# Two heads' scores at once in row halves, with the selection as a multiplied mask, for the last two of four sequences

## The chip, the cores and the metric

The kernel runs on one core of a Trainium2 chip. The metric is the device time in microseconds (us) of one launch; the time before is the median of three runs, 265.23 us (264.53 to 265.60).

## What is computed

Two stages follow each other. The first is causal attention over 4 sequences (B) of 768 tokens (S), 8 heads (H) of 64 channels (D), in which each query may look only at six of the 24 chunks of 32 keys. Which six is decided by an upper bound for each chunk, from the smallest and the largest key of the chunk in each channel:

```python
k_min, k_max = min and max of k over each chunk of 32 keys
ub = sum over channels of max(q * k_min, q * k_max)        # one number for query and chunk
ub = where(chunk of the key <= chunk of the query, ub, -1e9)
top_chunks = the 6 chunks with the largest ub
scores = q @ k.T / 8, -1e9 where the chunk isn't selected or the key lies behind the query
attn = softmax(scores);  x = attn @ v                       # heads side by side: [3072, 512]
h = max(x @ w_in, 0)                                        # w_in  [512, 2048]
out = (h * h) @ w_out                                       # w_out [2048, 512]
```

The second stage, the last two lines, is a feed-forward part over all 3072 tokens. Inputs and output are float32; the kernel computes in bf16 with float32 sums.

## The kernel before

**Tiles and units.** A tile is 128 tokens, so a sequence has six (NT). The first tile of every sequence needs no selection, since it has only four chunks; `first_attention` does it for all four sequences early on, with plain causal attention. The other five tiles (NS) are done by pairs of heads: pair p is sequence p // 4 and heads 2 (p % 4) and 2 (p % 4) + 1, which lie in channels 0 to 63 and 64 to 127 of a 128-row tile. There are 16 pairs.

**Stage a of a pair (`stage_a`, L622)** prepares it. Keys and queries, transposed to channels x tokens (`kT`, `qT`), give the bounds: two reductions over chunks on VectorE (`kr`, L690), small matmuls (`ub`, L656 and L658), a mask for later chunks (`ubm`, L715), the eight largest of each row (`MAX8`, L664), and a comparison with the sixth (`selb`, L720), which gives 1 for each chunk that is *not* selected. That is transposed (`sT`) so that chunks lie on rows. For sequences 0 and 1 the transposes are matmuls on TensorE; for sequences 2 and 3 (BY_DMA = 2) keys, queries and `sT` are turned by DMA transposes on SP's queue (`turn_by_dma`, L395).

**How the selection enters the scores before.** The matrix of the scores has 88 rows: 64 channels and 24 rows for the chunks. In `kqs` ("kqc" in the profile) the 24 rows hold -32768 where the key lies in the chunk; in `qss` ("qsc") they hold the turned selection. So a score of a chunk that isn't selected gets -32768 added by the matmul itself. `kqs` and `qss` have four sets (NSET), used in turn by the pairs. For every pair, eight copies fill a set: the keys of each head (`kqc<-kT` or `kqc<-kt`), the queries (`qsc<-qT`, `qsc<-qt`), and four copies of the selection (`qsc<-sT`). They are done by VectorE, or by ScalarE where the plan says so (lines L291 and L289 in the profile, the two branches of `copy`).

**Stage b of a pair (`stage_b`, L759)** does one head after the other in five "banks" of 512 columns (BANKS): scores into one PSUM buffer `ps` (L775, two or so matmuls of 88 rows), the exponential into `e` on ScalarE (L797), the causal cut of the diagonal tiles on GpSimd (L755) or VectorE (L752), and the product with the values into `av` (L786; a 65th column of ones gives the sum of the row). After five banks `normalise` (L601) divides into `x`.

**The feed-forward part (`ffn`, L816)** runs once for the four first tiles together and once for the five other tiles of each sequence: tokens are turned (`xT`), multiplied with `w_in` (`ph`, L859), passed through relu (`ht`, L866 on ScalarE or L868 on VectorE), squared (`h`, L877), multiplied with `w_out` (`py`, L890), copied to `ob` and written out by SP (L903).

**What sets the order.** Nothing loops at run time. `Plan` collects every operation with the engines that it may run on, an estimated cost, a due time, what it needs and which buffers it uses, and then places one operation after the other: the one that can start first, and among those on one engine that can start within 0.01 us of it, the one with the earliest due time. Buffers of a tag are taken from a fixed number of slots (three `ps`, two `av`, six `e`, three `ob` and so on) when their first user starts, and given back after the last. The result is one fixed order of instructions for each engine; at run time an engine only waits for semaphores. GpSimd's queue (POOL) issues the loads that convert float32 to bf16, in the order in which they were declared; SP's queue issues transposes by DMA and the output. Due times come from a few numbers in `P` (`lead` for each pair, `due` and `rate` for the feed-forward parts); `shift` can move the due time of single operations and is empty. Until 30 us the plan fills idle time of TensorE with matmuls on a constant (`wt`, L537).

Of the kernel before, what the change touches and what calls it, by code (L numbers as in the profile page):

```python
# [218 lines left out]
def kernel(  # L219
# [30 lines left out]
    P = dict(lead=[29, 46, 59, 39, 24, 71, 13, 53, 78, 15, 28, 72, 60, 6, 47, 77],  # L250
             f_due=[165, -158, -474.97, -240.97], sp='K0 Q0 K1 Q1', rows=-1719,
             rows_after=0, up_due=-70.08, up_rate=7.25, half=4,
             due=[-19, -136, -15, 35], rate=[4.42, 7.43, 6.24, 5.06], va=12.05,
             vm=6.24, ra=0.55, h2=-1.49, later='k1 q1 v1 k2 q2 q3 v2 v3 k3', shift={},
             p0=-3220, wait=0.01,
             loads="Q3 k0 K3 q0 V0 V1 V2 K2 Q2 k1 i0 "
                   "V3 i3 q1 v0 i2 k2 v1 R2 q2 i1 v2 o0 q3 k3 o1 v3 o2 o3")
# [13 lines left out]
    psav = ctx.enter_context(tc.tile_pool(name="psav", bufs=1, space=PSUM))  # L271
    psf = ctx.enter_context(tc.tile_pool(name="psf", bufs=1, space=PSUM))

    plan = Plan({"tp": 1, "ps": 3, "av": 2, "ff": 2, "e": 6, "h2": NFI + 6, "ht": 3,
                 "ob": 3, "kq": 6, "nt": 6,
                 "vn": B - 1, "x": 2, "xT": 2,
                 "kr": 2, "qp": 2, "qm": 2, "ubm": 2, "m8": 2, "rc": 2}, lambda *a: keep_warm(*a), P["wait"])
    POOLS = {"tp": pst, "ps": pss, "av": psav, "ff": psf, "e": epool, "h2": hpool,
             "ht": hpool, "ob": opool, "vn": ld, "nt": ldt, "kq": tpool}
# [13 lines left out]
    def transpose(dst, src):  # L293
# [10 lines left out]
    kqs = consts.tile([KC, NSET, 2, S], BF16, tag="kqs", name="kqc")  # L304
    qss = consts.tile([KC, NSET, 2, QC], BF16, tag="qss", name="qsc")
    selbs = consts.tile([128, NSET, NT, 2, 32], BF16, tag="selbs", name="selb")
    kbds = consts.tile([128, NSET, 2, 2, NC], BF16, tag="kbds", name="kbd")
    firsts = {nm: consts.tile([128, B, H, D], BF16, tag=nm + "0", name=nm + "0")
              for nm in "kq"}
# [3 lines left out]
    x_first = work.tile([128, B, d_model], BF16, tag="x0", name="x0", bufs=1)  # L313
# [17 lines left out]

    def make_ubmask(_):

        last = (NS - 1) * 128 // CH
        behind = consts.tile([128, last + NC], F32, tag="behind")
        nc.vector.memset(behind, 0.0)
# [7 lines left out]
    def kq_rows(i):  # L344
# [5 lines left out]
        elif i == 1:  # L350
            nc.sync.dma_start(out=kqs[D:KC, 0, 1], in_=kqs[D:KC, 0, 0])
        else:
            nc.gpsimd.dma_start(
                out=kqs[D:KC, 1:].rearrange("c s hh j -> c (s hh) j"),
                in_=kqs[D:KC, 0, 0:1].to_broadcast([NC, 2 * NSET - 2, S]))
# [16 lines left out]
    def first_of(nm, b):  # L372
        return vfirst[:, b, :, 0:D] if nm == "v" else firsts[nm][:, b]
# [613 lines left out]
```

## Time and profile before

The profile is of one execution. Its span, from the first to the last instruction, is 262.1 us; the median of the runs is 265.23 us, so 3.1 us lie outside the span.

| | before |
|---|---|
| median of the runs (lowest, highest) | 265.23 us (264.53, 265.60) |
| span of the profiled execution | 262.1 us |
| DMA packets, bytes | 103733, 26.12 MB |
| queue of POOL (software), of SP (hardware): MB | 13.33, 12.36 |
| granted clock of TensorE | full in each slice |

How to read the lines of the profile: PE is TensorE's matmuls, PEld its weight loads, DVE VectorE, ACT ScalarE, POOL GpSimd, SP the queue that only issues transfers. A group is written as line, engine, operation, written tile <- read tiles, shapes and count, then the busy time in us and the mean of one in ns, then the idle time of the engine just before them and what ended it. A matmul's busy time includes its way through the array, so that consecutive ones overlap; what each costs is seen from how far apart they start. The chain of work that ended last is followed back from the last instruction, and its lines say for how long what was on it. In the windows, "DMA share" is the busy time of the transfers over that of sixteen engines; where two queues are active, it can be above 1.

### The profile page before, as it was taken

To read this page: it belongs to the slowest core of one execution; us is meant where nothing else is said; L and a number is where in the kernel's file an instruction comes from. 1 tells how busy PE (TensorE), PEld (TensorE's weight loads), DVE (VectorE), ACT (ScalarE), POOL (GpSimd) and SP (SyncE) were. 2 spreads that over 40 slices of the span, in tenths; PEclk is the share of its full clock that TensorE was granted. 3 is DMA by queue.
4 is the path that set the end of the run, shared out by engine and by line. 5 is a ranking of instruction groups with operands and counts; after the bars stand their busy time and mean duration, and the time that the engine had idled before them with its cause. 6 is when DMAs were issued, how large, how long until landed. Compare 5 with 4: busy or idle time off the path is not lost.

```text
span 262.1 us, 6645 instructions
## 1 busy us (share of the span) xinstructions
PE 254.6 (97%) x2435; PEld 168.2 (64%) x2457; DVE 192.2 (73%) x677; ACT 180.2 (69%) x369; POOL 109.4 (42%) x196
## 2 busy tenths in 40 slices
PE   8899999999999999999999999999999999999995
PEld 4678765756687666656786656657767576565443
DVE  5399999968999999999999995886778531254000
ACT  1589798856599888986799847768889351377112
POOL 8997999978416729993121011411103000000000
PEclk9999999999999999999999999999999999999999
DMA  8999999999982999999571011163000011200222
GB/s 134 168 176 187 143 186 166 185 155 195 185 119 46 115 129 175 145 153 134 102 147 57 0 56 43 59 120 94 0 3 0 3 40 40 84 1 0 83 80 80
DMA packets 103733, 26.12 MB, mean 100 GB/s; under 512 B 96332, under 2 KB 100708, under 8 KB 103700
## 3 DMA queue, kind: packets, MB, share of 16 engines
q0 software_dynamic: 75168, 13.33, 65.9%
q1 hardware_dynamic: 28532, 12.36, 22.2%
q8 instruction: 19, 0.31, 0.5%
q14 instruction: 14, 0.11, 0.1%
HBM read 27.26 MB, written 6.29 MB: 128 GB/s over the span
## 4 chain that ended last, share of the span: by engine, by line
PE 89%; ACT 3%; DMA 3%; DVE 2%; issue 1%; SPq 1%; POOL 0%; ACTq 0%; POOLq 0%
PE py L890 31%; PE ph L859 31%; PE ps L775 13%; PE av L786 7%; DMA raw<-in_q_dram 3%; PE wt L537 1%; PE xt L294 1%; ACT qsc L289 1%; ACT ht L866 1%; PE kT L294 1%; SPq L406 1%; PE ub L658 1%; DVE kr L690 1%; PE ub L656 1%; PE qT L294 1%
## 5 line engine op out<-in xcount | busy, mean ns | idle before, releaser
L859 PE MATMUL ph<-xT,w_in_sb 128*128 128x256 bf16 (+2 forms) x592 | 98.0, 304 | 0.5 <-ACT ht L866 0.2
L797 ACT ACTIVATE e<-ps 128x512 bf16<-128x512 f32 x160 | 86.6, 604 | 10.8 <-PE ps L775 6.3
L890 PE MATMUL py<-w_out_sb,h 128*128 128x512 bf16 (+2 forms) x378 | 88.2, 370 | 1.2
L755 POOL TENSOR_SCALAR_AFFINE_SELECT e<-e 128x128 bf16<-128x128 bf16 (+1 forms) x102 | 34.8, 353 | 88.4 <-ACT e L797 79.7
L859 PEld LDWEIGHTS <-w_in_sb 128*128 128x128 bf16 x592 | 55.4, 97 | 24.5 <-issue 1.8
L866 ACT ACTIVATE ht<-ph 128x256 bf16<-128x256 f32 (+2 forms) x122 | 54.9, 455 | 17.2 <-PE ph L859 13.5
L877 DVE TENSOR_TENSOR h<-ht 128x256 bf16<-128x256 bf16 (+2 forms) x148 | 47.4, 330 | 19.9 <-ACT ht L866 13.1
L890 PEld LDWEIGHTS <-h 128*128 128x128 bf16 x400 | 36.5, 98 | 33.1
L775 PE MATMUL ps<-qsc,kqc 88*128 88x128 bf16 (+1 forms) x320 | 54.4, 272 | 0.0
L289 ACT COPY ob<-py 128x512 f32<-128x512 f32 (+2 forms) x22 | 12.5, 568 | 37.3 <-PE py L890 37.2
L786 PEld LDWEIGHTS <-e 128*128 128x128 bf16 x640 | 31.8, 97 | 7.9 <-POOL e L755 0.9
L775 PEld LDWEIGHTS <-kqc 88*128 88x128 bf16 x320 | 27.0, 98 | 11.9 <-issue 0.2
L786 PE MATMUL av<-vn,e 128*128 128x65 bf16 x480 | 32.0, 193 | 0.2 <-POOL e L755 0.2
L606 DVE TENSOR_TENSOR x<-av,rc 128x320 bf16<-128x320 f32 (+1 forms) x40 | 18.6, 470 | 0.3
L690 DVE TENSOR_REDUCE kr<-kT 128x24 bf16<-128x768 bf16 x16 | 14.8, 948 | 1.4 <-PE kT L294 1.4
L664 DVE MAX8 m<-ubm 128x8 f32<-128x24 f32 x160 | 15.6, 169 | 0.0
L690 DVE TENSOR_REDUCE kr<-kt 128x24 bf16<-128x768 bf16 x16 | 14.9, 944 | 0.0
L868 DVE TENSOR_SCALAR ht<-ph 128x256 bf16<-128x256 f32 (+2 forms) x26 | 12.2, 471 | 3.7 <-PE ph L859 3.6
L289 ACT COPY qsc<-sT 24x384 bf16<-24x384 bf16 (+1 forms) x32 | 14.1, 440 | 0.8
L786 PE MATMUL av<-v,e 128*128 128x65 bf16 x160 | 14.0, 193 | 0.0
L454 POOL DMA_DIRECT2D vn<-in_v_dram x15 | 13.3, 901 | 0.5 <-issue 0.5
L537 PE MATMUL wt<-warm 128*128 128x256 bf16 x73 | 11.5, 301 | 1.1 <-DVE warm L358 1.1
(84 smaller groups left out, 251.3 us busy)
## 6 DMA issues: line engine op xcount, KB each, us to landing
out_dram<-ob SPq DMA_DIRECT2D x23, 256.0 KB, 2.3
w_in_sb<-in_moe_w_in_dram POOLq DMA_DIRECT2D x4, 512.0 KB, 7.6
w_out_sb<-in_moe_w_out_dram POOLq DMA_DIRECT2D x4, 512.0 KB, 8.3
vn<-in_v_dram POOLq DMA_DIRECT2D x15, 128.0 KB, 5.7
nt<-in_k_dram POOLq DMA_DIRECT2D x10, 128.0 KB, 5.4
nt<-in_q_dram POOLq DMA_DIRECT2D x10, 128.0 KB, 5.7
kn<-in_k_dram POOLq DMA_DIRECT2D x8, 80.0 KB, 6.7
qn<-in_q_dram POOLq DMA_DIRECT2D x8, 80.0 KB, 6.7
```

The lines of the kernel that those rows point to most:

```text
L289: nc.scalar.copy(dst, src)
L606: return plan.op({"DVE": 0.06 + 0.00108 * D * n}, due, lambda _: nc.vector.tensor_mul(x(), av[:, :, 0:D], rc[:, 0:n].unsqueeze(2).to_broad ...
L664: nc.vector.max(out=m8[:, i, hh], in_=ubm[:, i, hh])
L690: nc.vector.tensor_reduce(kr[:, mm].rearrange("d (t c) -> d t c", c=128 // CH) if b >= BY_DMA else kr[:, mm], part(kT).rearrange("d t (c j ...
L755: nc.gpsimd.affine_select(out=e, in_=e, compare_op=ALU.is_ge, fill=0.0, base=0, channel_multiplier=-1, pattern=[[0, n], [1, 128]])
L775: nc.tensor.matmul(ps[:, 128 * c:128 * (c + nt)], lhsT=kqs[:, s, hh, 128 * j:128 * (j + 1)], rhs=qss[:, s, hh, 128 * (t0 - 1):128 * (t0 - ...
L786: nc.tensor.matmul(av[:, t - 1], lhsT=e[:, 128 * c:128 * (c + 1)], rhs=value_tile(b, h, j), start=(i == 0 and c == 0), stop=(i == len(BANK ...
L797: nc.scalar.activation(e.tile, ps.tile, ACT.Exp, scale=scale), [sc], [ps, e])
L859: nc.tensor.matmul(ph.tile, lhsT=w_in_sb[:, ki, 128 * f:128 * (f + 1)], rhs=xT[:, c0 // 128:c1 // 128, ki], start=(ki == 0), stop=(ki == N ...
L866: nc.scalar.activation(ht.tile, ph.tile, ACT.Relu)
L877: {"DVE": 0.067 + w / 1920}, at[0] + P["h2"], lambda _: nc.vector.tensor_mul(h2[f][:, c0:c1], ht.tile, ht.tile), [op], [ht, h2[f]])))
L890: nc.tensor.matmul(py.tile, lhsT=h2[f][:, 128 * t:128 * (t + 1)], rhs=w_out_sb[:, f, c0:c1], start=(f == 0), stop=(f == NFI - 1))
```

## The change

In sequences 2 and 3 (pairs 8 to 15), `stage_b_rows` takes the place of the loop over heads in `stage_b`.

- *Scores.* There is no `kqc` and no `qsc` for these pairs. The matmuls read the turned keys and queries directly, 64 rows for each head: the first head in rows 0 to 63, the second in rows 64 to 127, one after the other for every stretch of columns, each into a PSUM buffer of its own. They come in three groups (HELD): banks 0 and 1 of both heads, banks 2 and 3, bank 4. A group of two banks takes all three `ps` buffers and the `tp` buffer.
- *Selection.* `selb` holds 1 for a selected chunk now (is_ge for is_lt). It is turned by a DMA transpose of two instead of three blocks, written to DRAM by a DMA (`rowm`), and read back by six DMAs on SP's queue, one for each key tile, each of which copies four rows (the four chunks of the key tile) to 32 partitions each. The result is `keep`: 20 tiles of keys x queries for two heads. GpSimd cuts the five diagonal tiles of it causally. The reads of a pair wait for the last read of the pair before (`held_back`).
- *Product.* VectorE multiplies each `e` of 128 x 512 by its part of `keep` after the exponential; the causal cut of `e` goes for these pairs.
- *Room.* `kqs` and `qss` have three sets (KSET) instead of four. `keep` has two slots, in which at first the keys of the first tiles (`k0`) and the queries and results of the first tiles (`early`, before: `q0` and `x_first`) lie. There are eight `e` instead of six. The working tile of the mask for later chunks shares a slot of `ubm`.
- *Plan.* All numbers of `P` are new, `shift` now moves the due time of several hundred operations, and a list `order` rearranges the loads of POOL's queue.

Sequences 0 and 1 keep their way, apart from the three sets.

```diff
-    P = dict(lead=[29, 46, 59, 39, 24, 71, 13, 53, 78, 15, 28, 72, 60, 6, 47, 77],
-             f_due=[165, -158, -474.97, -240.97], sp='K0 Q0 K1 Q1', rows=-1719,
...
+    KSET = 3
+    P = dict(lead=[46.02, 34.36, 108.93, 41.94, 64.67, 97.83, 15.78, 50.83, 92.8, 36.24, 8.03,
+             91.81, 72.42, -35.47, 51.43, 62.87],
...
+             shift={2: -0.6, 6: -4.6, 7: -0.7, 10: -5.4, 11: -6.1, 12: -2.7, 14: -3.7, 15:
...
+             order=[4, 14, 1, 3, 5, 2, 0, 12, 6, 26, 9, 17, 10, 16, 8, 13, 7, 35, 11, 19, 15,
...
-    plan = Plan({"tp": 1, "ps": 3, "av": 2, "ff": 2, "e": 6, "h2": NFI + 6, "ht": 3,
+    plan = Plan({"tp": 1, "ps": 3, "av": 2, "ff": 2, "e": 8, "h2": NFI + 6, "ht": 3,
...
+                 "rowm": 8, "keep": 2, "kr": 2, "qp": 2, "qm": 2, "ubm": 2, "m8": 2, "rc": 2}, ...
...
+    early = buffer("keep", [128, 2, B, H, D], name="early")
+    firsts = {"k": buffer("keep", [128, B, H, D], name="k0"), "q": early}
...
         sel = op({"DVE": 0.32}, t0 + 19, lambda _: nc.vector.tensor_tensor(
...
-            op=ALU.is_lt), m + prepared.get((p - NSET, "sT"), []), [ubm, m8])
+            op=ALU.is_ge if b >= BY_DMA else ALU.is_lt), m + ..., [ubm, m8])
...
+    def spread(p, t, sT, rowm, due):
+
+        m = keep[p]
+        held_back = kept_before[-1:]
+        out = plan.op({"SP": 0.5}, due, lambda _: nc.sync.dma_start(
+            out=rowm.tile.rearrange("c t hh q -> (c t) hh q"),
+            in_=sT.tile[0:NC * NS]), [t], [sT, rowm], packets=130, turns=True, late=1.0)
+        kept = {}
+        for j in range(NT):
+            n = NT - max(1, j)
+            kept[j] = plan.op({"SP": 0.5}, due + 1 + 0.1 * j, lambda _, j=j, n=n: nc.sync.dma_start(
+                out=m[:, ROW[j]:ROW[j] + n].rearrange("k t hh q -> k (t hh q)"),
+                in_=rowm.tile[4 * j:4 * j + 4, max(1, j) - 1:NS].rearrange(
+                    "a t hh q -> a (t hh q)").unsqueeze(1).to_broadcast(
+                        [4, 32, 256 * n])),
+                [out] + held_back, [rowm, m], packets=170 * n, turns=True, late=1.0)
+        kept_before.append(kept[NT - 1])
+        prepared[p, 0] = prepared[p, 1] = []
+        prepared[p, "keep"] = [kept[0]] + [plan.op(
+            {"POOL": 0.36}, due + 2, lambda _, j=j: causal("POOL", m[:, ROW[j]], 2),
+            [kept[j]], [m]) for j in range(1, NT)]
...
+    TILES = [(j, t) for j in range(NT) for t in range(max(1, j), NT)]
+    ROW = {j: min(i for i, u in enumerate(TILES) if u[0] == j) for j in range(NT)}
+    HELD = [(0, 1), (2, 3), (4,)]
+    HEADS = [tuple(TILES[4 * i:4 * i + 4]) for i in range(len(TILES) // 4)]
...
+    def stage_b_rows(p, x):
...
+            def scores(_, banks=banks, pss_=pss_):
+                for i in banks:
+                    c = 0
+                    for j in range(NT):
+                        ts = [t for jj, t in HEADS[i] if jj == j]
+                        if not ts:
+                            continue
+                        for hh in range(2):
+                            rows = slice(D * hh, D * hh + D)
+                            nc.tensor.matmul(
+                                pss_[i, hh][:, 128 * c:128 * (c + len(ts))],
+                                lhsT=kT[rows, j, hp],
+                                rhs=qT[rows, ts[0] - 1:ts[-1], hp],
+                                start=True, stop=True)
+                        c += len(ts)
...
+                    mu = plan.op({"DVE": 0.334}, due + P["vm"], lambda _, e=e, i=i, hh=hh:
+                                 nc.vector.tensor_mul(
+                                     e.tile.rearrange("k (t q) -> k t q", q=128),
+                                     e.tile.rearrange("k (t q) -> k t q", q=128), m[:, 4 * i:4 * i + 4, hh]),
+                                 [ex] + prepared[p, "keep"], [e, m])
...
```

More of the change, by code (lines that the diff above doesn't have):

```diff
@@ L330, in make_ahead @@
             channel_multiplier=-1, pattern=[[1, 128]])
+    behind = buffer("ubm", [128, (NS - 1) * 128 // CH + NC], F32, name="behind")
     def make_ubmask(_):
         last = (NS - 1) * 128 // CH
-        behind = consts.tile([128, last + NC], F32, tag="behind")
-        nc.vector.memset(behind, 0.0)
+        nc.vector.memset(behind.tile, 0.0)
         for g in range(4):
@@ L448, in load_turned @@
             lambda: dst[:, i],
-            lambda: (src.tile if src else firsts[nm][:, b]).rearrange(
-                "p h d -> p (h d)"), due, needs, [src, dst], late=4.5)
+            lambda: (src.tile if src else tokens_of(nm, b)).rearrange(
+                "p h d -> p (h d)"), due, needs, [src or firsts[nm], dst], late=4.5)
         loaded.setdefault((nm, b), []).append(op)
@@ L496 @@
     ones(0, -980)
-    made["ubmask"] = plan.op({"DVE": 0.8}, -997, make_ubmask)
+    made["ubmask"] = plan.op({"DVE": 0.8}, -997, make_ubmask,
+                             tiles=[behind])
     for what in P["loads"].split():
@@ L625, in stage_a @@
         t0 = HALVES * p - P["lead"][p] if p else P["p0"]
[L626 removed]
+        ks = p % KSET
+        before = scored.get(p - KSET, [])
         if b >= BY_DMA:
@@ L951 @@
             down(NS - 1, 384)
-    computed = [op for op in plan.ops if op.turns or not op.packets]
     for i, change in P["shift"].items():
-        computed[i].due += change
+        plan.ops[i].due += change
+    plan.loads = [plan.loads[i] for i in P["order"]]
     with tc.manual_schedule():
```

140 lines of the change are left out of this document (102 added, 38 removed), and 147 rows, old and new, of tables (order, shift).

## The prediction

> **What bounds the kernel now.** I read the page's busy line and chain first, then the windows, then single stretches of the chain. The busy line and the two lines of the chain:
>
> ```profile
> PE 254.6 (97%) x2435; PEld 168.2 (64%) x2457; DVE 192.2 (73%) x677; ACT 180.2 (69%) x369; POOL 109.4 (42%) x196
> ...
> PE 89%; ACT 3%; DMA 3%; DVE 2%; issue 1%; SPq 1%; POOL 0%; ACTq 0%; POOLq 0%
> PE py L890 31%; PE ph L859 31%; PE ps L775 13%; PE av L786 7%; DMA raw<-in_q_dram 3%; PE wt L537 1%; PE xt L294 1%; ACT qsc L289 1%; ACT ht L866 1%; PE kT L294 1%; SPq L406 1%; PE ub L658 1%; DVE kr L690 1%; PE ub L656 1%; PE qT L294 1%
> ```
>
> The reader is to see that TensorE is the bound by work, not by waits: 89% of the chain is PE. Scores (`ps L775`) are 13% of it. The windows (length; busy time and count of PE, PEld, DVE, ACT, POOL; clock; DMA share; GB/s) say the same by stage:
>
> ```profile
> 104.00:124.00 20.00, 19.83 (x234) 12.85 (x236) 19.52 (x59) 16.89 (x34) 15.93 (x31) 1.00 1.86 145
> 124.00:150.00 26.00, 25.92 (x231) 18.19 (x231) 24.36 (x97) 22.56 (x53) 4.06 (x12) 1.00 0.37 80
> 150.00:205.00 55.00, 54.37 (x576) 36.69 (x579) 42.77 (x151) 41.14 (x84) 10.49 (x31) 1.00 0.18 45
> 205.00:262.00 57.00, 53.79 (x332) 30.73 (x335) 14.34 (x43) 20.48 (x44) 0.00 (x0) 1.00 0.13 47
> 220.00:230.00 10.00, 9.95 (x60) 5.38 (x60) 2.77 (x10) 2.91 (x7) 0.00 (x0) 1.00 0.18 68
> ```
>
> From 104 to 205, PE is busy 100.1 of 101 us, at full clock. VectorE is nearly full until 150 and has some 12 us free from 150 to 205. The DMA engines are crowded until 124 (share 1.86) and nearly free afterwards. After 205 only the feed-forward part is left and every other engine has room. So work taken off PE is time gained, as long as nothing makes PE wait.
>
> **The scores.** A stretch of the chain (start, us, what, count) and the scores by window:
>
> ```profile
> 88.66 0.65 PE ph L859 x4
> 89.31 0.44 PE ps L775 x4
> 89.75 0.12 PE av L786 x4
> 89.87 0.86 PE py L890 x4
> ```
>
> ```profile
> 115.00:204.00 89.00, 26.78 (x160) 13.89 (x160) 1.00 0.39 65
> ```
>
> Four score matmuls (two banks of 512 columns) take 0.44 us of PE. The last 160, those of pairs 8 to 15, the ones that change, lie between 115 and 204: 11.1 us a pair. By their part of the chain (13% of 262.1 us, half of it) they cost 17.0 us. What two heads in row halves cost is seen in the first-tile attention, which already does this with 128 columns:
>
> ```profile
> 13.50 0.44 PE L294 MATMUL qT<-ident,qn 128*128 128x128 bf16 x5
> 13.87 0.40 PE L573 MATMUL ps<-t,t 64*128 64x128 bf16 x8
> 14.20 0.27 PE L580 MATMUL av<-v,e 128*128 128x65 bf16 x3
> ```
>
> ```profile
> L573 PE MATMUL ps<-t,t 64*128 64x128 bf16 x32 | 1.6, 219 | 0.0
> ```
>
> One such matmul lasts 0.22 us alone, so five in 0.44 us start 0.055 us apart, while the eight of L573 in 0.40 us start 0.026 us apart: two run at once. But L573 starts at 13.87 where the next start was due at 13.78, and L580 at 14.20 where it was due at 14.08: about 0.22 us are lost in going over to the halves and back. The change makes three such groups a pair (HELD), 24 in all. So: half of 17.0 is 8.5, plus 24 x 0.22 = 5.2, makes 13.7 us, **3.3 us less PE work**. Had the switch cost nothing it would be 8.5 less; were nothing paired, 5.2 more.
>
> **VectorE, ScalarE, GpSimd.** Groups of the whole run, and, of the stretch 115 to 205, the wider half of the mask copies that pairs 8 to 15 lose (busy, mean ns):
>
> ```profile
> L797 ACT ACTIVATE e<-ps 128x512 bf16<-128x512 f32 x160 | 86.6, 604 | 10.8 <-PE ps L775 6.3 <-PE av L786 3.6 <-POOL e L755 0.4
> ...
> L755 POOL TENSOR_SCALAR_AFFINE_SELECT e<-e 128x256 bf16<-128x256 bf16 x24 | 10.1, 421 | 12.1 <-ACT e L797 11.8 <-DVE h L877 0.2
> ...
> L291 DVE COPY qsc<-qt 64x640 bf16<-64x640 bf16 x16 | 7.6, 475 | 0.3
> ...
> L291 DVE COPY kqc<-kt 64x768 bf16<-64x768 bf16 x16 | 6.5, 409 | 0.2
> ...
> L877 DVE TENSOR_TENSOR h<-ht 128x512 bf16<-128x512 bf16 x12 | 5.0, 437 | 0.3 <-ACT ht L866 0.2
> ```
>
> ```profile
> L291 DVE COPY qsc<-sT 24x384 bf16<-24x384 bf16 x6 | 2.1, 344 | 0.2
> ```
>
> The 80 multiplications by the mask are of the shape of `h<-ht`: 80 x 0.437 = 35.0 us of DVE. The copies that go are at least 7.6 + 6.5 + 2.1 = 16.2 us, so DVE gains at most 18.8 us, and 86.7 of 101 us between 104 and 205 become 105.5. I charge nothing: some relus can go to ACT, which keeps its 80 exponentials at 604 ns (48 us) but loses its share of the mask copies, and what remains can run after 205, where DVE has 42 us free while PE has feed-forward work of the last two sequences. Without that cover it costs the 4.5 us that don't fit. GpSimd's five selects a pair at 0.42 us replace its selects on `e`; it is idle from 124 on, so nothing. KSET 3 for 4 gives the copies of pairs 3 to 7 less lead; nothing, as PE has other work at hand there.
>
> [...]
>
> **The masks.** This decides the sign. Each pair now needs a transpose, a write to DRAM, six reads that copy it to 128 partitions, five selects, then the products. A pair's mask is 20 tiles x 2 heads x 128 x 128 in bf16: 1.31 MB. DMA rows (KB each, median us from issue to landing) and the queue of SP around it:
>
> ```profile
> out_dram<-ob SPq DMA_DIRECT2D x23, 256.0 KB, 2.3
> ...
> kqc<-kqc POOLq DMA_DIRECT2D x1, 216.0 KB, 5.9
> ...
> sT<-selb SPq DMA_TRANSPOSE x8, 2.3
> out_dram<-ob SPq DMA_DIRECT2D x1, 64.0 KB, 1.6
> ```
>
> ```profile
> 104.80 1.18 SPq L396 DMA_TRANSPOSE sT<-selb  x1
> ...
> 125.46 1.26 SPq L396 DMA_TRANSPOSE kt<-k  x1
> ```
>
> ```profile
> 179.51 80.24 SPq L903 DMA_DIRECT2D out_dram<-ob  x12
> ```
>
> After 179.51 only output writes are in flight, and the window 220 to 230 moved 68 GB/s at a share of 0.18: 378 GB/s for sixteen busy engines. At that rate a mask takes **3.5 us**, the low end. The one broadcast in this trace, `kqc<-kqc` on POOL's queue (24 rows, each copied six times), took 5.9 us for 216 KB in a crowd; less 1.4 us that any transfer takes (1.6 us less what 64 KB need), a mask would take **26.7 us**, the high end. That row is the nearest in kind, but its crowd had the share that the rows before 124 have, near 1.8, so some 15 us without it. A second way: each read names only four rows of DRAM, and if four rows keep a quarter of the engines busy it is 13.9 us. I take **13.9**.
>
> A read set of a pair may not begin before the one ahead has landed (held_back), so sets follow each other at 13.9 + 1.4 = 15.3 us, against 11.1 us in which PE now does a pair. The first selection leaves at 104.80; transpose 2.3 and write 1.6 put the first read at 108.7, and eight sets end at 108.7 + 122.4 = 231.1. Then select, product, values and normalising, about 2 us (estimate from the 0.42 and 0.44 above), then all of the last sequence's feed-forward part, which needs every head: 64 weights x 640 columns at 0.65 us for 4 x 384 are 17.3 us, and 80 matmuls at 0.86 us for four are 17.2. That is 267.6. The last 3.0 us follow by this row of the chain, where the last `py` ends at 259.06 of 262.1:
>
> ```profile
> 250.86 8.20 PE py L890 x53
> ```
>
> So the span is 270.6, and with the 3.1 us by which the median of the runs (265.2) lies above the profiled span, **274 us**. PE's own work, 262.1 - 3.3 = 258.8, is then not the bound; PE idles some 12 us, because its instructions stand in a fixed order and the values of a pair hold up the feed-forward work behind them. On SP, 56 new issues at about 0.33 us are 18 us of room that it has; but what waits behind a read that waits for its buffer are the output writes, three `ob` buffers deep, and the transposes of `x` and of the next selection, and behind those PE again.
>
> Bounds on this: a set that takes 12.4 us or less costs nothing, since 108.7 + 8 x 13.8 + 2 + 34.5 + 3.0 meets 258.8. Sets in the crowd before 124 go at half pace, 13.9 us more at worst, 288. The second mask buffer is the old `k0`, whose last reader in this trace is the transpose at 125.46, another 4 us.
>
> [...]
>
> **The refit.** Nearly every due time and the order of the loads are new. The profile cannot price that. What it could win are the fillers on PE while it waits for first loads, of which this is the longest group after 17 us:
>
> ```profile
> 20.11 1.15 PE L537 MATMUL wt<-warm 128*128 128x256 bf16 x9
> ```
>
> Nine cost about 1 us; I take nothing, and keep 3 us to either side.
>
> **The rivals.**
> - *Masks hidden* (other side, chance 0.33). The reads use all engines, or sets stay below 12.4 us. Then PE's 3.3 us are the result: 261.9, from 258.5 with a good refit to 263.9. For it: after 124 the DMA engines are idle, and selections lead their scores. Against: the only broadcast in the trace is slow.
> - *Emptying or VectorE takes the gain* (0.10): a group of two banks holds four PSUM buffers until four exponentials, 2.4 us, are through, and DVE must find 18.8 us. Against: both have room after 150. 264 to 266.5.
> - *The halves don't run at once for 512 columns* (0.03): 5.2 more PE work, 270.4. Against: L573.
>
> **How the numbers follow.** Forecast *masks late*: 0.54, own range 266.5 to 288. Half a per cent, 1.3 us, is what a measurement of this kernel can tell from no change. Faster by more: 0.33; within: 0.10; slower: 0.54 + 0.03 = 0.57. The range for 8 in 10 reaches from 259.5, leaving out the best refits, to 288.
>
> **What would show it.** Right, if PE shows gaps before `av` between 115 and 235, released by DVE's products and those by the mask reads; if the six reads of a pair land 13 to 16 us after the first is issued; if the last scores and values end near 230. The scores' part holds if 24 groups of row halves take 13.7 us of PE. Wrong, if the reads of a pair land within 6 us, or PE stays above 97% busy from 104 to 205: then it is the first rival.

## The result, and the profile after

The changed kernel takes 317.44 us (median of 4 runs, 316.14 to 318.87) where the kernel before took 265.28 us in the same job (4 runs): a ratio of 1.198, with a 95% interval from 1.193 to 1.204. The forecast was 274.0, with a range up to 288.0. The sign was right, the size was not. The profiled execution took 317.71 us, with a span of 316.0. Of all runs below, one was in a slower state of the chip (281.21 us, in the last experiment) and is left out there.

The page of the changed kernel: busy time, the slices of PE and of its clock, the engines' shares of the chain, and the groups of the selects and of the products.

```profile
PE 263.9 (83%) x2426; PEld 163.4 (52%) x2450; DVE 200.5 (63%) x699; ACT 178.6 (57%) x357; POOL 109.1 (35%) x178
...
PE   7899999999999999379728735979929496999996
...
PEclk9999999999999999969969785999986988999999
...
PE 42%; DMA 27%; DVE 11%; SPq 10%; ACT 5%; issue 3%; POOL 1%; POOLq 0%; DVEq 0%; ACTq 0%
...
L966 POOL TENSOR_SCALAR_AFFINE_SELECT keep<-keep 128x256 bf16<-128x256 bf16 x40 | 19.2, 481 | 129.5 <-DMA keep<-rowm 102.9
...
L1069 DVE TENSOR_TENSOR e<-e,keep 128x512 bf16<-128x512 bf16 x80 | 31.3, 430 | 47.8 <-DMA keep<-rowm 22.9
```

TensorE fell from 97% busy to 83%, and from 89% of the chain to 42%; transfers and SP's queue hold 37% of it now. PE's slices are full up to the sixteenth and have holes from there on, and the clock falls in and behind the holes (digits down to 5). The products themselves cost 430 ns each, forecast from `h<-ht` at 437; it is the waits ahead of them that are new.

The windows of the changed kernel (length; busy time and count of PE, PEld, DVE, ACT, POOL; clock; DMA share; GB/s) show where it begins:

```profile
100.00:120.00 20.00, 19.73 (x197) 11.77 (x199) 18.93 (x66) 16.34 (x35) 12.20 (x20) 1.00 1.95 172
120.00:150.00 30.00, 22.80 (x202) 14.35 (x202) 18.81 (x71) 14.27 (x32) 2.20 (x5) 0.89 0.55 110
150.00:200.00 50.00, 29.40 (x263) 15.88 (x267) 24.66 (x72) 18.15 (x35) 6.40 (x15) 0.80 0.27 98
200.00:250.00 50.00, 39.24 (x342) 22.41 (x340) 29.69 (x114) 27.96 (x57) 8.20 (x14) 0.93 0.51 111
```

Up to 120 us TensorE is as busy as in the kernel before. From 120 on, when the first mask is read, TensorE does 91.4 us of work in 130, at a granted clock of 0.80 to 0.93. The waits (us in total, times, longest):

```profile
POOL keep L966 <- DMA keep<-rowm: 102.9, 35, 16.3
...
PEld L1076 <- DVE e L1069: 40.2, 10, 9.2
...
DVE e L1069 <- DMA keep<-rowm: 22.9, 3, 8.7
DVE e L1069 <- POOL keep L966: 22.0, 4, 10.0
```

This is the forecast's path: select waits for the read, product for the select or the read, the values' weight load for the product, in ten waits of up to 9.2 us. SP's queue (start, us until the last of them is issued, count) shows a second thing. The single line behind it is of another view and gives the least, median and longest time in ns that one of the 48 reads takes to be issued:

```profile
113.91 0.36 SPq L924 DMA_DIRECT2D rowm<-sT  x1
...
117.84 3.33 SPq L564 DMA_TRANSPOSE xT<-x  x2
121.27 7.45 SPq L930 DMA_DIRECT2D keep<-rowm  x6
128.77 7.73 SPq L564 DMA_TRANSPOSE xT<-x  x3
136.54 2.54 SPq L564 DMA_TRANSPOSE sT<-selb  x2
...
147.00 21.57 SPq L930 DMA_DIRECT2D keep<-rowm  x12
...
171.13 9.62 SPq L930 DMA_DIRECT2D keep<-rowm  x6
...
191.61 7.54 SPq L930 DMA_DIRECT2D keep<-rowm  x6
...
219.54 36.59 SPq L930 DMA_DIRECT2D keep<-rowm  x18
```

```profile
L930 SPq DMA_DIRECT2D keep<-rowm x48: 517/824/6447, 121.3 to 253.6; - x48
```

Twelve reads hold the queue for 21.57 us and eighteen for 36.59; the 48 together hold it for 82.8. Nothing else leaves SP in that time: no turned `x`, no turned selection, no output. It isn't `held_back` that does this. That list only enters the plan, which puts the operations in order; at run time no wait of a read for the landing of the set ahead shows. What SP waits for before its reads, in the whole run (us in total, times, longest), is the write of the selection, and, little, the buffer:

```profile
SPq L930 <- DMA rowm<-sT: 10.8, 3, 8.2
...
SPq L930 <- DVE e L1069: 3.4, 1, 3.4
```

Otherwise the 82.8 us are the issuing itself: 0.52 to 0.61 us for each of the first three reads from 121.27, 147.00, 191.61 and 219.54 on, and up to 6.45 us for those that stand behind them. When a set has landed is seen from the select on its last key tile (start, us, then the wait before it):

```profile
137.56 0.42 POOL L966 TENSOR_SCALAR_AFFINE_SELECT keep<-keep 128x256 bf16<-128x256 bf16 x1 [0.86 <-DMA keep<-rowm]
...
191.35 0.41 POOL L966 TENSOR_SCALAR_AFFINE_SELECT keep<-keep 128x256 bf16<-128x256 bf16 x1 [2.85 <-DMA keep<-rowm]
...
208.71 0.51 POOL L966 TENSOR_SCALAR_AFFINE_SELECT keep<-keep 128x256 bf16<-128x256 bf16 x1 [0.39 <-DMA keep<-rowm]
```

So the first set takes 16.3 us (121.27 to 137.6), the next three 44.4 (147.00 to 191.4), the fifth 17.1 (191.61 to 208.7), and the last three 44.5 (219.54 to the last select at 264.0). That is 122.2 us for eight sets, where the forecast had 122.4. But they aren't back to back: no set is under way for 9.4 us before 147.00 and for 10.8 us before 219.54, while SP sends what had been held up, the next selections among it.

### The profile page after: what moved, and what is told of

It reads as the page before. It is cut to its first block, busy times and chain, and to the rows that moved or that the text cites. A ratio compares the mean times of both kernels' runs of the same rounds, so it can differ in the third digit from the quotient of the medians.

```text
span 316.0 us, 6661 instructions
## 1 busy us (share of the span) xinstructions
PE 263.9 (83%) x2426; PEld 163.4 (52%) x2450; DVE 200.5 (63%) x699; ACT 178.6 (57%) x357; POOL 109.1 (35%) x178
## 4 chain that ended last, share of the span: by engine, by line
PE 42%; DMA 27%; DVE 11%; SPq 10%; ACT 5%; issue 3%; POOL 1%; POOLq 0%; DVEq 0%; ACTq 0%
DMA keep<-rowm 22%; PE py L1167 16%; PE ph L1136 14%; SPq L930 7%; PE ps L988 4%; DVE kr L865 3%; DMA xT<-x 2%; DMA raw<-in_q_dram 2%; PE av L999 2%; ACT qsc L452 2%; DVE e L1069 2%; SPq L564 2%; PE av L1076 1%; DMA rowm<-sT 1%; DVE h L1154 1%
## 5 line engine op out<-in xcount | busy, mean ns | idle before, releaser
L1167 PE MATMUL py<-w_out_sb,h 128*128 128x512 bf16 (+2 forms) x376 | 92.2, 382 | 1.6 <-issue 0.4
L1143 ACT ACTIVATE ht<-ph 128x384 bf16<-128x384 f32 (+2 forms) x119 | 53.9, 459 | 35.3 <-PE ph L1136 20.0
L966 POOL TENSOR_SCALAR_AFFINE_SELECT keep<-keep 128x256 bf16<-128x256 bf16 x40 | 19.2, 481 | 129.5 <-DMA keep<-rowm 102.9
L1069 DVE TENSOR_TENSOR e<-e,keep 128x512 bf16<-128x512 bf16 x80 | 31.3, 430 | 47.8 <-DMA keep<-rowm 22.9
L1154 DVE TENSOR_TENSOR h<-ht 128x256 bf16<-128x256 bf16 (+2 forms) x148 | 47.9, 334 | 13.7 <-ACT ht L1143 11.5
L1076 PE MATMUL av<-v,e 128*128 128x65 bf16 x80 | 7.2, 220 | 38.0 <-DVE e L1069 34.9
L988 PE MATMUL ps<-qsc,kqc 88*128 88x128 bf16 (+2 forms) x160 | 25.4, 272 | 0.4 <-ACT e L1010 0.2
L966 POOL TENSOR_SCALAR_AFFINE_SELECT e<-e 128x128 bf16<-128x128 bf16 (+1 forms) x44 | 14.9, 342 | 22.5 <-ACT e L1010 14.7
L1076 PE MATMUL av<-vn,e 128*128 128x65 bf16 x240 | 15.2, 210 | 2.6 <-DVE e L1069 2.6
L988 PEld LDWEIGHTS <-kqc 88*128 88x128 bf16 x160 | 13.3, 97 | 6.3 <-issue 0.9
L775 DVE TENSOR_TENSOR x<-av,rc 128x320 bf16<-128x320 f32 x32 | 15.3, 486 | 0.4
L838 DVE MAX8 m<-ubm 128x8 f32<-128x24 f32 x160 | 15.3, 174 | 0.0
```

Of the source, the lines that this page charges most:

```text
L966: nc.gpsimd.affine_select(out=e, in_=e, compare_op=ALU.is_ge, fill=0.0, base=0, channel_multiplier=-1, pattern=[[0, n], [1, 128]])
L988: nc.tensor.matmul(ps[:, 128 * c:128 * (c + nt)], lhsT=kqs[:, ks, hh, 128 * j:128 * (j + 1)], rhs=qss[:, ks, hh, 128 * (t0 - 1):128 * (t0 ...
L1069: nc.vector.tensor_mul(e.tile.rearrange("k (t q) -> k t q", q=128), e.tile.rearrange("k (t q) -> k t q", q=128), m[:, 4 * i:4 * i + 4, hh]),
L1076: nc.tensor.matmul(avs[hh][:, t - 1], lhsT=e[:, 128 * c:128 * (c + 1)], rhs=value_tile(b, 2 * hp + hh, j), start=(i == 0 and c == 0), stop ...
L1143: nc.scalar.activation(ht.tile, ph.tile, ACT.Relu)
L1154: {"DVE": 0.067 + w / 1920}, at[0] + P["h2"], lambda _: nc.vector.tensor_mul(h2[f][:, c0:c1], ht.tile, ht.tile), [op], [ht, h2[f]])))
```

## The experiments

The theory after the result had two parts. *Rate*: reads of four rows use a quarter of the transfer engines (the share is 0.27 from 150 to 200 us), so each mask is late. *Queue*: while the reads hold SP's queue, what stands behind them (turned `x`, turned selections, outputs) is late too. The rivals were that waiting for masks is the whole loss; that the new plan is at fault, fitted to reads that it takes for short; and that VectorE or the emptying of PSUM binds once the masks are there. Where one execution is given, it stands beside one or several of the kernel before on the same chip, named with it.

### Reads that name sixteen rows

The selection is written to DRAM four times, so that each read names sixteen rows of DRAM with eight partitions each, instead of four with 32.

```diff
-    rowm = buffer("rowm", [NC, NS, 2, 128], name="rowm")
+    rowm = buffer("rowm", [NC, 4, NS, 2, 128], name="rowm")
...
+            for u in range(4)], [t], [sT, rowm], packets=130, turns=True, late=1.0)
...
-                        [4, 32, 256 * n])),
+                        [16, 8, 256 * n])),
```

> The changed kernel with one difference: the mask lies in DRAM four times, so that each read names sixteen rows of it, eight partitions each, instead of four rows, thirty-two partitions each. Bytes read, order of all instructions and plan stay; three small writes a pair are added. Theory (the reads are slow because four source rows keep four engines busy): a pair's six reads land about 5 us after the first is issued instead of 13 to 16, PE no longer waits for products, 262 us (258 to 267). Rival (the order on SP's queue and the serial chain of transfers cost it, not the rate): the reads may be shorter, but the time stays above 295 us. Rival (broadcast reads are slow however they are cut): reads still 13 us or more, 317 us.

Measured: 283.07 us (281.53 to 283.46), ratio to before 1.068 (1.061 to 1.076). First the rate, by a window of each in which next to nothing but reads is in flight (columns as above): of the changed kernel,

```profile
148.00:160.00 12.00, 7.71 (x54) 4.26 (x52) 6.65 (x22) 5.88 (x12) 1.71 (x4) 1.00 0.25 88
```

and of the kernel with four copies:

```profile
150.00:157.00 7.00, 1.52 (x9) 0.68 (x7) 0.54 (x5) 1.48 (x4) 1.99 (x5) 0.99 0.83 240
205.00:213.00 8.00, 3.11 (x23) 1.72 (x22) 2.04 (x7) 2.46 (x5) 2.63 (x6) 0.91 0.95 257
```

Four rows keep a share of 0.25 busy and move 88 GB/s; sixteen rows keep 0.83 to 0.95 busy and move 240 to 257. So the rate part holds: 34.4 of the 52 us go with one change of shape. SP's queue bears it out a second way: twelve reads in a row hold it for 7.68 us here (149.26 to 156.94) and for 21.57 us there, and the longest issue of a read is 1.41 us here, 6.45 us there. But the 262 us (258 to 267) that I expected were missed by 21 us, and the first set takes 7.5 us, not 5. The runs show the shares and the rates; why four rows keep only 0.25 busy they don't show.

The rest shows in SP's queue of this kernel:

```profile
139.50 9.57 SPq L924 DMA_DIRECT2D rowm<-sT  x12
...
193.11 9.56 SPq L924 DMA_DIRECT2D rowm<-sT  x12
```

Three pairs are written in a row, twelve writes that hold the queue 9.6 us ahead of the reads.

### Products that don't wait for the mask

The products multiply the constant `tri` instead of the mask; writes, reads and selects stay.

```diff
-    e.tile.rearrange("k (t q) -> k t q", q=128), m[:, 4 * i:4 * i + 4, hh]),
+    e.tile.rearrange("k (t q) -> k t q", q=128),
+    tri.unsqueeze(1).to_broadcast([128, 4, 128])),
```

> The changed kernel, but the products multiply by a constant tile (the causal one, the same shape) instead of the pair's mask, so nothing waits for the reads; the reads, selects and the fixed order all stay. Leaves the selection out of the last two sequences. Theory (waiting for the masks is the whole loss): 262 to 268 us, with TensorE at full clock after 120 us, though the reads on SP's queue are as slow as before. Rival (the reads' traffic and SP's blocked queue also hold up loads, transposes and output): 285 us or more.

Measured: 309.33 us (one execution; before 263.91, median of 7). The rival that waiting for masks is the whole loss falls: without any wait for a mask only 8 us come back. Its waits:

```profile
ACT ob L452 <- DMA out_dram<-ob: 38.8, 3, 15.0
...
PE ph L1137 <- DMA xT<-x: 19.6, 2, 15.5
```

The copies to `ob` wait 38.8 us for outputs, and the feed-forward part 19.6 us for turned `x`, both of which are issued behind reads. SP's queue runs as in the changed kernel:

```profile
147.48 21.94 SPq L930 DMA_DIRECT2D keep<-rowm  x12
```

The last select starts at 264.2 us here and at 264.0 there. Three selections are ready at 175.6, 177.4 and 181.5 here and are turned only from 211.0 on, behind reads, outputs and turned `x`. So it isn't the products, which free the buffers of the mask, that hold the reads back. With slow reads, SP's queue alone costs nearly as much as queue and waits for masks together: the two overlap in the changed kernel.

### A plan that knows how long the reads take

```diff
-                [out] + held_back, [rowm, m], packets=170 * n, turns=True, late=1.0)
+                [out] + held_back, [rowm, m], packets=830 * n, turns=True, late=1.0)
```

> The changed kernel with the plan told what the reads cost: 830 instead of 170 units for each key tile's width, so that the order of the instructions is made for slow reads. The transfers themselves stay. Theory (the serial reads of 15 us a pair are a bound by themselves): order helps by little, 300 us (290 to 312). Rival (only the fixed order, made for fast reads, costs the time): 265 to 280 us.

Measured: 303.95 us (one execution; before 263.91). 13.5 us come from another order, with the same transfers, as the theory had it. The wrong estimate in the plan is a part of the loss, not its cause.

### Four copies with the plan of before

Four copies as above; all numbers of `P` are those of the kernel before, without `shift` and without `order`.

```diff
-    plan.loads = [plan.loads[i] for i in P["order"]]
```

> The kernel of the first experiment (four copies in DRAM) with the plan's numbers of the kernel before: no shifts, the old leads, due times and order of loads. Against the first experiment it gives the price of the refit. Theory (the refit is needed with the new operations, and is worth some per cent): 270 to 276 us, against about 262 with the new numbers. Rival (the refit is worth nothing): within 1.5 us of the first experiment.

Measured: 278.56 us (one execution; before 263.91), 4.5 less than with the new numbers. The refit was expected to be worth some per cent and was worth less than nothing here: neither the 270 to 276 us of the theory nor the "within 1.5 us" of the rival.

### Reads on GpSimd's queue

The six reads of a pair are issued by GpSimd, with four rows as in the changed kernel.

```diff
-            kept[j] = plan.op({"SP": 0.5}, due + 1 + 0.1 * j, lambda _, j=j, n=n: nc.sync.dma_start(
+            kept[j] = plan.op({"SP": 0.5}, due + 1 + 0.1 * j, lambda _, j=j, n=n: nc.gpsimd.dma_start(
```

> The changed kernel with the six mask reads of a pair issued on GpSimd's queue instead of SP's; each still names four rows of DRAM. SP keeps the transposes, the write of the mask and the output. Theory (two losses: the reads' own 13 to 16 us a pair, and what stands behind them on SP's queue): the second goes, the first stays, 290 to 305 us, PE waiting for products and no longer for xT, ACT no longer for output. Rival (the rate alone): no change within 4 us of 317. Rival (SP's blocked queue alone): 270 us or less.

Measured: 294.79 us (one execution; before 264.42), 22.6 us less than the changed kernel. The number was forecast, but the run doesn't separate the two parts, since the reads become faster as well. Its window 150 to 200, with a share of 0.56, where the changed kernel has 0.27:

```profile
150.00:200.00 50.00, 44.17 (x405) 23.96 (x407) 39.52 (x137) 27.46 (x56) 21.93 (x37) 0.90 0.56 129
```

By the selects again, the eight sets take 98 us instead of 122, while the gaps between them are no smaller (24 us instead of 20.5). What a free queue for SP is worth at the old rate stays open here; the queue part rests on the run without waits for the mask, above, and on the next one.

### Four copies, writes on GpSimd's queue

```diff
-        out = plan.op({"SP": 0.5}, due, lambda _: [nc.sync.dma_start(
+        out = plan.op({"SP": 0.5}, due, lambda _: [nc.gpsimd.dma_start(
```

> Four copies in DRAM as in the first experiment (283), but the four small writes of a pair go by GpSimd's queue, so SP's queue has only the six reads that the change gave it. Theory (what the first experiment still loses is SP's time for twelve writes in a row, 9.6 us ahead of the reads of the second and sixth pair): 266 to 273 us. Rival (the reads are still too slow for the plan even on all engines): 280 us or more.

Measured: 268.78 us (one execution; before 264.42). Its busy line, its clock, and its window 150 to 200:

```profile
PE 252.2 (94%) x2426; PEld 157.6 (59%) x2450; DVE 202.3 (76%) x699; ACT 177.9 (67%) x357; POOL 130.6 (49%) x210
...
PEclk9999999999999999999999999999999999999999
```

```profile
150.00:200.00 50.00, 47.55 (x465) 27.16 (x467) 42.20 (x146) 33.31 (x69) 20.60 (x37) 1.00 0.67 177
```

The holes are gone, and so is the loss of clock. The same 2426 matmuls are busy for 252.2 us, and for 263.9 in the changed kernel: the difference, 11.7 us, is about what the lower clock makes of them (worked out further below). Against the first experiment, 14.3 us come back with the reads as fast as there, by taking the writes off SP's queue.

### Four copies, writes and reads on GpSimd's queue

Both edits together, so that SP's queue has nothing of the mask but the transposes.

> Four copies in DRAM, with both the writes and the reads of the masks on GpSimd's queue; SP's queue is as short as in the kernel before. Theory: 262 to 270 us, at most as long as with the reads on SP. Rival (GpSimd's slower issue, about 0.9 us each, or its waits in order hold up its selects): 275 us or more.

Measured: 272.31 us (one execution; before 264.42), 3.5 more than with the reads on SP, and between the theory (262 to 270) and the rival (275 or more). With fast reads SP's queue is no worse a place for them than GpSimd's.

### No transfers of the mask at all

Write, reads and selects go, and the products multiply `tri`: what is left of the change is the scores in halves, the products, the three sets, and the plan.

```diff
-        out = plan.op({"SP": 0.5}, due, lambda _: nc.sync.dma_start(
+        out = plan.op({"SP": 0.5}, due, lambda _: None, [t], [sT, rowm], packets=130, ...
...
-            kept[j] = plan.op({"SP": 0.5}, due + 1 + 0.1 * j, lambda _, j=j, n=n: nc.sync.dma_start(
+            kept[j] = plan.op({"SP": 0.5}, due + 1 + 0.1 * j, lambda _: None,
...
-            {"POOL": 0.36}, due + 2, lambda _, j=j: causal("POOL", m[:, ROW[j]], 2),
+            {"POOL": 0.36}, due + 2, lambda _, j=j: None,
```

> The changed kernel without the write to DRAM, the six reads and the selects on them; the products multiply by a constant tile of the same shape. Leaves the selection out of the last two sequences. All other instructions and their order stay. Theory (the scores' 3.3 us less PE work are real and everything lost is lost by the transfers): 259 to 263 us with PE busy 97%. Rival (VectorE's 80 products or the four held PSUM buffers are a second bound): 266 us or more.

Measured: 263.01 us (one execution; before 264.42). Its busy line and a window, and its matmuls around one score group of each kind (L1045: banks 2 and 3, bank 4, banks 0 and 1):

```profile
PE 251.7 (96%) x2426; PEld 157.9 (60%) x2450; DVE 199.2 (76%) x699; ACT 177.2 (68%) x357; POOL 89.7 (34%) x138
```

```profile
150.00:200.00 50.00, 49.62 (x508) 29.05 (x514) 43.90 (x152) 35.92 (x75) 0.00 (x0) 1.00 0.20 46
```

```profile
159.78 1.67 PE L1162 MATMUL py<-w_out_sb,h 128*128 128x512 bf16 x7
161.38 0.61 PE L1045 MATMUL ps<-qt,kt 64*128 64x256 bf16 x8
161.93 0.33 PE L1071 MATMUL av<-v,e 128*128 128x65 bf16 x5
...
163.66 1.03 PE L1162 MATMUL py<-w_out_sb,h 128*128 128x512 bf16 x4
164.62 0.40 PE L1045 MATMUL ps<-qt,kt 64*128 64x128 bf16 x6
164.95 0.42 PE L1071 MATMUL av<-vn,e 128*128 128x65 bf16 x8
...
167.55 2.75 PE L1162 MATMUL py<-w_out_sb,h 128*128 128x512 bf16 x12
170.24 0.61 PE L1045 MATMUL ps<-qt,kt 64*128 64x512 bf16 x6
170.78 1.47 PE L1162 MATMUL py<-w_out_sb,h 128*128 128x512 bf16 x6
```

VectorE (43.90 of 50) and ScalarE (35.92) don't bind, and TensorE is busy for 49.62 of 50: the rival of emptying and VectorE falls. The groups last 0.55, 0.33 and 0.54 us from their start to the next instruction. Ahead of them, 7, 4 and 12 `py` at 0.215 (0.86 for four) take 0.10, 0.10 and 0.11 us longer than their columns need. That makes 1.73 us for this pair, 13.8 us for eight like it: the forecast was 13.7. The time itself is 1.4 us below that of the kernel before, one execution each, and within the spread of that kernel (263.51 to 266.44 in 19 runs).

### The same without the new order of the loads, and with all numbers of before

Two runs price the refit where no mask is in the way; the first leaves `order` out, the second takes all of `P` from the kernel before.

> No write, no reads and no cut of the mask (the selection is left out, each product multiplies a constant), as in the run that gave 263.0, but the loads of GpSimd's queue in the order of before. Theory (the refit's order of the loads makes the start about 2.5 us worse, which hides most of the 3.3 that the scores give): 260 to 262, and the first stretch of the trace ends about 2 earlier. Rival (the scores give less than 3.3 and the start is the same): 263 or more.

> No write, no reads and no cut of the mask (the selection is left out), with all numbers of the plan of before, no shifts and the old order of the loads. Theory (the scores give 3.3 of TensorE's work, the start is that of before): 260 to 264, the upper part if the numbers of before fit the new operations badly. Rival (the refit is worth much where no mask is waited for): 266 or more.

Measured: 266.55 us (264.94 to 268.20, 10 runs), ratio 1.006 (1.003 to 1.010); and 272.73 us (270.79 to 273.20, 4 runs), ratio 1.029 (1.024 to 1.035); before 265.18 (19 runs). My reading that the new order of the loads spoils the start was wrong: without it the kernel isn't faster. The busy line of the second:

```profile
PE 256.6 (94%) x2435; PEld 160.7 (59%) x2457; DVE 200.7 (74%) x698; ACT 178.6 (66%) x358; POOL 90.0 (33%) x138
```

TensorE is idle for 14.9 of 271.5 us there, and for 9.6 of 261.3 with the new numbers. Both times are those of the rivals. The refit is worth 9.7 us to the new operations where the masks cost nothing (against the one execution of 263.01). With four copies and the writes on SP it lost 4.5.

### Attempts at a version that wins

Four copies with the writes on GpSimd's queue; the durations of the transfers in the plan set to about what the traces show; and either the numbers of before, or numbers refitted to these durations with the kernel's own planner:

```diff
+    P.update(lead=[29, 46, 59, 39, ...], due=[-19, ...], rate=[4.42, ...], va=..., vm=..., ra=..., h2=...)
...
-                [out] + held_back, [rowm, m], packets=170 * n, turns=True, late=1.0)
+                [out] + held_back, [rowm, m], packets=250 * n, turns=True, late=1.2)
```

> Four copies, writes on GpSimd's queue, the numbers of the plan of before without shifts, and the planner told about the true durations of the transfers. Theory (the queue of SP and the share of the transfer engines were the loss, the refit is of little worth here): 266 to 273. Rival (the refit is what makes 268.8 possible): 274 or more.

> Four copies of the mask, so that a read names sixteen rows; the writes on GpSimd's queue; the numbers of the plan refitted by the kernel's own planner with about the durations that the traces show for the transfers (a read 250 units a block, a write 520 units in all), starting from the numbers of before, without the shifts and without the list for the loads. Theory (the transfers and the order of the plan around them are all that costs): at or a little below the 268.8 of the run with the writes on GpSimd's queue, 263 to 269; it beats before only if the refit gives more than 4. Rival (something else in the change costs some microseconds, so that no order saves it): 269 or more.

Measured: 277.02 us (276.89 to 278.59, 3 runs), ratio 1.049 (1.042 to 1.055), and 266.82 us (265.65 to 268.56, 10 runs), ratio 1.0075 (1.0043 to 1.0108); before 265.18 (19 runs). So a refit made for these transfers is worth 10.2 us here, which the first of the two expectations had denied. The best version found is still 0.75% slower than the kernel before. The busy line of that version:

```profile
PE 254.0 (96%) x2433; PEld 159.0 (60%) x2457; DVE 199.8 (75%) x678; ACT 182.3 (69%) x371; POOL 131.0 (49%) x217
```

TensorE is idle for 10.9 of 264.9 us, and for 7.5 of 262.1 before: 3.4 us more in small waits. And it is busy for only 0.6 us less than before (254.0 against 254.6), where the run without masks had 2.9 less; why so little is left of that stays open.

## Why the prediction was right and wrong

**What bounds the kernel; the scores; VectorE: right.** Work on TensorE was the bound, 13.8 us of scores (from one pair) against 13.7 forecast, 430 ns a product against 437, and no second bound at VectorE or at the emptying of PSUM. (GpSimd isn't idle from 124 on, as I wrote: its rows have 4.06 and 10.49 us to 205. It bound nothing.) Of the 3.3 us less work on TensorE, its busy time shows 2.9 (251.7 us without the masks, 254.6 before). With the numbers of the plan of before it is 256.6, at a mean clock of 0.987 against 0.992, so busy time isn't the work alone: the order and the clock are in it too. In the time of the run without masks 1.4 us show, one execution each, and not clear of the spread. Where the rest goes stays open; that the order of the loads hides it, as I had suspected, isn't borne out.

**The likeliest case: right in kind.** The masks come late, at a quarter of the engines (shares of 0.25 to 0.27), and TensorE stands before `av`. Of the signs, the gaps before `av` and the 13.7 us of scores came true; the first set lands 16.3 us after its first read is issued, just outside the 13 to 16, and the last values end near 269, not 230. The rival *masks hidden* would need reads on all engines; even with these (four copies, shares of 0.83 to 0.95) the kernel was slower than before. So the bound that a set of 12.4 us or less costs nothing doesn't hold either: the first set takes 7.5 us there, and the kernel still loses 19 us (283.07 against 263.91).

**The sum: wrong by 45.4 us of span (316.0 against 270.6).** The sum chains 108.7, eight sets of 15.3, and 39.5 to the end. Its terms as measured:

| term | forecast | measured | off by |
|---|---|---|---|
| first read issued | 108.7 | 121.3 | 12.6 |
| from there until the last read has landed (eight sets) | 122.4 | 142.7 | 20.3 |
| from there to the end | 39.5 | 52.0 | 12.5 |

The failed step is the room on SP's queue: "56 new issues at about 0.33 us are 18 us of room that it has". The 48 reads alone hold the queue for 82.8 us, since a read that stands behind others takes up to 6.45 us to be issued. The prediction went on to name what waits behind (output writes, transposes of `x` and of the next selection, "and behind those PE again"), and charged nothing for it.

- *First read.* It leaves after the transposes of `x` that stand before it in the order (117.84), and its write (113.91) waits in the same queue. I took 104.80 from the profile before and let nothing stand between.
- *Eight sets.* The 13.9 us of a set rest on my estimate that four rows keep a quarter of the engines busy, which no trace of the kernel before shows. In the changed kernel the share is 0.25 at 88 GB/s (148 to 160 us), and a set takes 14.8 to 17.1 us. The sets themselves take 122.2 us, as forecast, but that is in part luck. `held_back`, which the prediction and the description of the change take for a wait at run time, is none; sets overlap where they follow each other (14.8 us each, by threes) and take 16.3 and 17.1 us alone. The 20.5 us of gaps are the miss. In the first, the next two selections, ready at 125.9 and 128.5, are turned only from 136.54 on, behind three transposes of `x`, which stand behind the reads.
- *End.* I let only the feed-forward work of the last sequence follow. In the trace, 43 `py` of an earlier part stand behind the last products in TensorE's fixed order and run from 265.4 to 277.5. With fast reads (four copies, writes on GpSimd's queue) it is 54.2 us from the last select to the end (212.9 to 267.1). So this term belongs to the order of the changed kernel, not to late masks.

How much of the loss is rate and how much is queue can't be told apart: the slower read is also the slower to issue (up to 6.45 us, with sixteen rows up to 1.41). Three runs give sizes. Faster reads on SP's queue bring 34.4 us; reads on the other queue, which are faster too, bring 22.6; and without any wait of a product for its mask 45 us of loss remain (309.33 against 263.91).

**Second omission: the clock.** I took the granted clock as full throughout, as in the profile before. In the changed kernel it falls from 1.00 to 0.50 in or behind holes, and the same matmuls take 11.7 to 12.2 us longer (263.9 against 252.2 and 251.7). That fits: in seven stretches from 133 to 270 us, 41.0 us in all, the granted clock is 0.50 and TensorE is busy for 25.5. In one of them four `ph` of 384 columns take 1.26 us up to the next instruction (164.19 to 165.45), in the kernel before 0.65 at full clock (88.50 to 89.15). So at full clock about half of the 25.5 would do, and some 12.7 us are the clock's (an estimate from these windows). No run held TensorE busy in the holes, so what that would give back is argued, not shown.

**The refit, taken as nothing: wrong as an estimate, and of no account for the forecast.** It is worth 9.7 us to the new operations without masks, and another refit, made for fast reads, 10.2 us; with four copies and the writes on SP it costs 4.5. Relative to the kernel before it only keeps the time level (263.01 against 264.42).

**Outside the span.** I added 3.1 us; the profiled execution has 1.7 (317.71 less 316.0). The runs of the kernel before have 1.7 as well where time and span are of the same run (263.84 and 262.1); the 3.1 compares a span with the median of other runs.

The ledger from the run without masks to the changed kernel, in the order in which the runs undo it: 263.0; 268.8 with masks read by all engines and written by GpSimd (5.8); 283.1 with the writes on SP (14.3); 317.4 with reads of four rows (34.4, rate, queue and clock together). In another order the shares would differ: moving the four-row reads off SP alone gives 22.6.

## What to carry to other kernels

A transfer that is slow to issue, or waits, is charged to its whole queue (here 48 reads held SP's for 82.8 us): list what stands behind it and who waits for that, before adding up transfer times. Look at how many rows of DRAM a transfer names; here sixteen instead of four took the share from 0.25 to 0.83 and more, and was worth 34 us of 317 at the price of three more small writes. And in a kernel bound by TensorE, look at the clock as well as at the idle time when a wait lasts several microseconds: here waits of 6.64 to 8.89 us had a clock of 0.50 in them and behind them.

## What the runs showed of the hardware

Not expected was how the clock answers to holes. A window of the changed kernel in which TensorE hardly works, and one that begins in it:

```profile
155.00:163.00 8.00, 0.71 (x5) 0.19 (x2) 0.00 (x0) 0.98 (x2) 1.23 (x3) 0.83 0.26 97
```

```profile
161.00:167.00 6.00, 3.02 (x17) 1.68 (x18) 3.51 (x14) 1.57 (x3) 0.00 (x0) 0.50 0.27 103
```

In the 8 us to 163 TensorE has 0.71 us of work, and the mean clock is 0.83; from 161 to 167 it is 0.50 throughout, so it has fallen within the hole (TensorE's wait of 8.27 us for a product, up to 163.97) and stays low for the first work behind it. The same shows at its waits of 6.88, 8.89 and 6.64 us, up to 136.49, 193.01 and 237.67, while the clock stays at 1.00 around the wait of 2.06 us up to 212.49. In the run with four copies and the writes on GpSimd's queue, the weight loads of TensorE wait for products at most 1.5 us at a time,

```profile
PEld L1077 <- DVE e L1070: 6.8, 13, 1.5
```

and the clock stays at 9 in every slice.

Nor was it expected that reads of four rows are faster on GpSimd's queue than on SP's: 129 GB/s at a share of 0.56 against 98 at 0.27 from 150 to 200 us, and, looked at more closely, 115 to 149 GB/s at shares of 0.46 to 0.58 while a set is under way (windows 144 to 155, 166 to 177, 178 to 189, 204 to 216 and 226 to 239 of the run with the reads there), against 86 to 97 GB/s at 0.25 to 0.26 (windows 148 to 160, 155 to 163 and 220 to 236 of the changed kernel).
